# Batch 0's FFN evictions and the maxima of the second mixing get positions of their own, and twelve differences of u move from GpSimd to VectorE

## The chip, the cores and the metric

The kernel runs on one core of a Trainium2 chip. The core has five engines, each with an in-order queue of its own: TensorE (PE) for matrix products, VectorE (DVE), ScalarE (ACT) and GpSimd (POOL) for everything on rows, and SyncE (SP), which here issues the DMAs. Engines wait for each other through semaphores. The metric is the device time of one execution in microseconds (us), the median of several runs.

## The reference

```
scores = scale * q @ k^T - log(S)            # 8 batches, 12 heads, S = 448, head dim 64
x      = sigmoid(scores) @ v                 # back in the shape batch, S, 768
h      = x^T @ U @ V                         # U: 448 x 32, V: 32 x 448, mixes along S
u      = x + h^T
out    = u + relu(u @ w_ch1) @ w_ch2         # 768 -> 3072 -> 768
```

All inputs and the output are float32. The sigmoid attention is followed by a low-rank mixing along the sequence and by an FFN, each with its residual.

## The kernel before

A batch goes through three stages. The attention makes x, kept transposed as six tiles of 128 channels x 448 positions (`ua` for batch 0, `ub` for batch 1 and others). The mixing (`mix`) transposes x (L736), multiplies it by U (L758) and by V (L777) and adds the result to the same tiles, which then hold u. After each addition `largest` (L457) takes the maximum of a tile into `mx`; when all six are there, `mm_u` (L848) reduces them and PE spreads the result over the partitions (L409), from which comes a power-of-two scale. The FFN works in float16 pairs: each operand is split into a high and a low part, and a product is done as three matmuls, hi x hi, hi x lo, lo x hi.

Batches 0 to 3 run the FFN as it stands, in six groups of four hidden slices. `ffn_in` is a chain of 18 matmuls (L914) into a PSUM bank; ACT evicts it twice with a relu (`r`, L921, and the high part `h`, L922), and DVE makes the low part (L923). `ffn_out` is a chain of 12 matmuls (L933) into a bank, which one DVE instruction (a SCALAR_TENSOR_TENSOR of the helper in L393) adds, scaled, to the tile `ua__75` to `ua__80` of u. The two kinds of chain share three banks, 109, 110 and 111, with each other and with the spreading of maxima (L409). So a chain begins when the evictions of the bank's last chain are done.

While batch 0 is in its FFN, much else runs: `decode` brings the weights in, from DMA tiles `w` through ACT (L442), DVE (L393, on 128x768 int32, into `us__88`, `stg` or `at`), a sum on ACT (L453), and high and low parts (L886 on ACT, L393 on DVE) into `w__89` to `w__92`; and batch 1 goes through attention and mixing (`mix(1)`).

Batches 4 to 7 do the FFN in the pairs (4,5) and (6,7) by a scheme of seven products in place of eight on 2x2 blocks. `u_forms` makes the seven left operands from the u of the two batches, for each of three channel thirds c: it loads four blocks and scales them on ACT (L1070), makes the differences t1 to t4 (L1074), casts each operand to its high part on ACT (L1077) and subtracts this for the low part (L1079). `in_quad` multiplies them (L1117), evicts the sums on ACT (L1140) and DVE (L393), and makes the seven operands of the second product by differences (L1146), casts (L1154) and low parts (L1155); `out_quad` multiplies those (L1117 again). For the pair (6,7) the four differences and the low parts of two operands (n = 4 and 6) for each c are on POOL, 18 instructions.

The order of each engine's queue is not written by hand. Every piece of work is given to a `Plan` with an engine, an estimated cost and a position `pos`. `Plan.order` simulates the engines with those costs: an engine that is free takes, among the operations that are ready and have their buffers, the one with the lowest position. `plan.emit()` then writes the instructions in that order, once and for all. A position decides only between operations that are ready at the same simulated time. Evictions of `ffn_in` have the chain's position less `EV_IN` = 29.859, those of `ffn_out` less `EV_OUT` = 5.77.

Of the kernel before, what the change touches and what calls it, by code (L numbers as in the profile page):

```python
# [32 lines left out]
AF = mybir.ActivationFunctionType  # L33
# [35 lines left out]
W_AT, W_STEP, PAIR0, MIX0A, MIX0B, W2_LAG, G0_LEAD = -159.513, 4.417, 4.011, -137.936, -80.644, 0.347, 0.582  # L69
LOW_G = 1  # L70
ORDER = "iiiioiooiioiooiioiooiooo"

# [159 lines left out]
def fused_kernel(ctx: ExitStack, tc: tile.TileContext, q, k, v, wu, wv, w1, w2, out):  # L232
# [474 lines left out]
    def mix(b, pos0, pos1):  # L707
# [61 lines left out]
        for c in range(NP):  # L769
# [6 lines left out]
            else:  # L776
# [3 lines left out]
                    [lp, ku[c], kap], [ku[c]], at)  # L780
            largest(lambda c=c: u32[c].x, lambda c=c: mx.x[:, c : c + 1], [ku[c]], kmx[c], at)
        at += 0.5
# [121 lines left out]
    def ffn_in(b, g, f, pos):  # L904
# [6 lines left out]
        def chain():  # L911
            for c in range(NP):
# [7 lines left out]
        r = plan.tile("r", R)  # L920
        act(0.54, lambda: nc.scalar.activation(r.x, ph.x[:, :S], AF.Relu, scale=DOWN_H), [ph], [r], pos - EV_IN)  # L921
        act(0.54, lambda: nc.scalar.activation(h.x[:, f, 0, :], ph.x[:, :S], AF.Relu, scale=DOWN_H), [ph], [(h, f, 0)], pos - EV_IN)  # L922
        dve2(0.62, lambda: nc.vector.tensor_tensor(out=h.x[:, f, 1, :], in0=r.x, in1=h.x[:, f, 0, :], op=ALU.subtract),  # L923
             [r, (h, f, 0)], [(h, f, 1)], pos - EV_IN)

    def ffn_out(b, g, e, pos):
# [3 lines left out]
        def chain():  # L930
# [9 lines left out]
        dve(0.68, lambda: stt(ku.x, po.x[:, :S], kg.x[:, g : g + 1], ku.x, ALU.mult, ALU.add),  # L940
            [po, (kg, g), ku], [ku], pos - EV_OUT)
        if g == NG - 1:
# [119 lines left out]
    def u_forms(b0, b1, su, pos, after):  # L1062
        fs = {}
        for c in range(3):
# [8 lines left out]
            for o, p_, q_ in ((t1, x[0, 1], x[0, 0]), (t3, x[1, 1], x[0, 1]), (t2, x[1, 1], t1), (t4, x[1, 0], t2)):  # L1073
                pool(1.0, lambda o=o, p_=p_, q_=q_: nc.gpsimd.tensor_tensor(out=o.x, in0=p_.x, in1=q_.x, op=ALU.subtract), [p_, q_], [o], at)  # L1074
            for n, src in ((1, x[0, 0]), (2, x[1, 0]), (3, x[1, 1]), (5, t1), (7, t3), (6, t2), (4, t4)):
                f = fs[n, c] = spot("uf")
                act(0.57, lambda f=f, src=src: nc.scalar.copy(both(f)[:, 0], src.x), [src], [(f, 0)], at)  # L1077
                on_pool = n == 4 or n == 6
                (pool if on_pool else dve2)(1.2 if on_pool else 0.63, lambda f=f, src=src, e=nc.gpsimd if on_pool else nc.vector: e.tensor_tensor(  # L1079
                    out=both(f)[:, 1], in0=src.x, in1=both(f)[:, 0], op=ALU.subtract), [src, (f, 0)], [(f, 1)], at)  # L1080
# [297 lines left out]
```

## Time and profile before

| what | us |
|---|---|
| median of 3 runs | 1559.37 |
| the runs | 1556.81, 1559.37, 1562.81 |
| the profiled execution | 1556.6 |
| its span on the core | 1554.8 |
| PE busy, 0 to 100 us of the span | 91.52 |
| PE busy, 100 to 200 us | 98.51 |
| PE busy, 1300 to 1500 us | 200.00 |
| PE busy, 1500 us to the end | 51.11 of 54.80 |

In this kernel PE is nearly always busy, so time is read from where it is not. In a timeline row the columns are the start and the length in us, the engine, the line, the operation, out<-in with the names of tiles, the sizes, the number of instructions put together (x), and in brackets the idle time just before, with what ended it. Tiles are named by their buffer, which different data use in turn: `stg`, `a`, `w`, `at`, `us__87`, `us__88`, `qk`, `v`, `h` and `r` hold operands of the pair (6,7) late in the program and weights or activations before. A row by stretch gives the window, its length, the busy time and number of instructions of PE, weight loads, DVE, ACT and POOL, then the granted TensorE clock, the DMA share and GB/s.

### The profile page before, as it was taken

To read this page: it belongs to the slowest core of one execution; us is meant where nothing else is said; L and a number is where in the kernel's file an instruction comes from. 1 tells how busy PE (TensorE), PEld (TensorE's weight loads), DVE (VectorE), ACT (ScalarE), POOL (GpSimd) and SP (SyncE) were. 2 spreads that over 40 slices of the span, in tenths; PEclk is the share of its full clock that TensorE was granted. 3 is DMA by queue.
4 is the path that set the end of the run, shared out by engine and by line. 5 is a ranking of instruction groups with operands and counts; after the bars stand their busy time and mean duration, and the time that the engine had idled before them with its cause. 6 is when DMAs were issued, how large, how long until landed. Compare 5 with 4: busy or idle time off the path is not lost.

```text
span 1554.8 us, 24080 instructions
## 1 busy us (share of the span) xinstructions
PE 1524.8 (98%) x8843; PEld 749.9 (48%) x8843; DVE 1118.2 (72%) x1864; ACT 846.9 (54%) x1495; POOL 388.7 (25%) x538
## 2 busy tenths in 40 slices
PE   8999979999999999999999999999999899999999
PEld 3344534544444444444444454555555455555554
DVE  4787898666877768867686856787777667565656
ACT  6788766468867668687686627333332514131310
POOL 1100010642223563312235420055544500000000
PEclk9999999999999999999999999999999999999999
DMA  8877868674665766746766465966566483343331
GB/s 240 270 265 258 265 226 331 233 253 150 154 193 140 236 202 188 186 148 175 239 201 205 161 208 176 308 211 236 201 237 212 145 272 107 117 127 113 107 107 71
DMA packets 184726, 306.02 MB, mean 197 GB/s; under 512 B 54560, under 2 KB 146080, under 8 KB 178464
## 3 DMA queue, kind: packets, MB, share of 16 engines
q1 hardware_dynamic: 184608, 304.49, 61.8%
q8 instruction: 69, 1.13, 0.3%
q14 instruction: 49, 0.40, 0.1%
HBM read 232.88 MB, written 63.26 MB: 190 GB/s over the span
## 4 chain that ended last, share of the span: by engine, by line
PE 86%; DVE 5%; DMA 3%; ACT 3%; issue 1%; POOL 1%; SPq 0%; ACTq 0%; DVEq 0%; POOLq 0%
PE bank L1117 36%; PE bank L933 18%; PE bank L914 18%; PE bank L533 5%; PE bank L552 5%; DMA w<-w_in 3%; DVE stg L393 1%; PE bank L562 1%; PE bank L829 1%; PE bank L537 1%; ACT w L453 1%; DVE us__88 L393 1%; PE bank L838 0%; DVE at L393 0%; DVE w__90 L393 0%
## 5 line engine op out<-in xcount | busy, mean ns | idle before, releaser
L933 PE MATMUL bank<-h__94,w__92 128*128 128x448 f16 x864 | 175.1, 355 | 6.8 <-DVE ua__78 L393 6.8
L933 PE MATMUL bank<-h__93,w__91 128*128 128x448 f16 x864 | 173.5, 353 | 1.9 <-DVE ua__76 L393 1.1
L393 DVE SCALAR_TENSOR_TENSOR a<-at,a 128x896 f16<-128x896 f32 x126 | 137.5, 1112 | 27.5 <-ACT a L679 27.2
L933 PEld LDWEIGHTS <-w__92 128*128 128x128 f16 x864 | 83.0, 98 | 91.0 <-issue 18.6
L914 PEld LDWEIGHTS <-w__89 128*128 128x128 f16 x864 | 83.3, 98 | 84.7 <-issue 8.2
L933 PEld LDWEIGHTS <-w__91 128*128 128x128 f16 x864 | 82.3, 98 | 86.6 <-issue 13.9
L914 PEld LDWEIGHTS <-w__90 128*128 128x128 f16 x864 | 83.8, 98 | 82.0 <-issue 4.8
L679 ACT ACTIVATE a<-at 128x896 f16<-128x896 f32 x126 | 115.5, 960 | 0.6
L1117 PEld LDWEIGHTS <-w__90 128*128 128x128 f16 x756 | 74.4, 98 | 74.7 <-issue 6.7
L976 POOL TENSOR_TENSOR w<-w 128x384 f32<-128x384 f32 x96 | 107.4, 1118 | 5.1
L1117 PEld LDWEIGHTS <-w__92 128*128 128x128 f16 x756 | 74.0, 98 | 69.0
L1117 PEld LDWEIGHTS <-w__89 128*128 128x128 f16 x756 | 74.0, 98 | 69.0
L1117 PEld LDWEIGHTS <-w__91 128*128 128x128 f16 x756 | 74.0, 98 | 68.8
L914 PE MATMUL bank<-us__87,w__89 128*128 128x448 f16 x432 | 84.9, 353 | 2.2 <-DVE ua__78 L393 2.2
L914 PE MATMUL bank<-us__87,w__90 128*128 128x448 f16 x432 | 85.5, 353 | 1.3 <-ACT h__94 L922 1.3
L914 PE MATMUL bank<-us__88,w__89 128*128 128x448 f16 x432 | 85.6, 353 | 0.0
L914 PE MATMUL bank<-us__88,w__90 128*128 128x448 f16 x432 | 85.5, 353 | 0.0
L533 PE MATMUL bank<-stg 64*128 64x448 f16 x648 | 73.8, 351 | 0.0
L972 POOL TENSOR_TENSOR w<-w 128x384 f32<-128x384 f16 x48 | 45.1, 969 | 107.5 <-DVE xnt L984 74.8
L552 PE MATMUL bank<-a,stg 128*64 128x448 f16 x648 | 68.2, 355 | 0.0
L921 ACT ACTIVATE r__95<-bank 128x448 f32<-128x448 f32 x48 | 26.1, 544 | 69.4 <-PE bank L914 69.3
L649 ACT ACTIVATE at<-bank,bias_s,c__216 128x448 f32<-128x448 f32 x72 | 47.2, 726 | 22.8 <-PE bank L533 14.1
(1143 smaller groups left out, 3078.7 us busy)
## 6 DMA issues: line engine op xcount, KB each, us to landing
w<-w_in SPq DMA_DIRECT2D x48, 768.0 KB, 6.3
forms<-xnt SPq DMA_DIRECT2D x24, 768.0 KB, 4.1
w__89<-kept SPq DMA_DIRECT2D x9, 1536.0 KB, 6.5
w__91<-kept SPq DMA_DIRECT2D x9, 1536.0 KB, 9.4
w__90<-kept SPq DMA_DIRECT2D x9, 1536.0 KB, 6.9
w__92<-kept SPq DMA_DIRECT2D x9, 1536.0 KB, 8.3
w__89<-forms SPq DMA_DIRECT2D x12, 768.0 KB, 4.7
w__90<-forms SPq DMA_DIRECT2D x12, 768.0 KB, 5.5
```

Source lines behind the costliest of these rows:

```text
L393: nc.vector.scalar_tensor_tensor(out=out, in0=in0, scalar=s, in1=in1, op0=op0, op1=op1)
L453: act(cost, lambda: nc.scalar.activation((to.x.bitcast(BF16) if to else junk)[:, :n], x(), AF.Abs, accum_out=o()), kx, [ko] + ([to] if to ...
L533: nc.tensor.matmul(sc[j, h].x[:, :S], x[rows_of(h), j * P : j * P + P], y[rows_of(h)], start=i == 0, stop=i == n - 1)
L552: nc.tensor.matmul(av.x[rows_of(h), :S], x[:, j, rows_of(h)], y(tiles[j], h), start=j == 0 and i == 0, stop=not quad and j == 2 and i == n ...
L649: act(cost, lambda: nc.scalar.activation(out_(), in_(), AF.Sigmoid, bias=bias_s, scale=c if whole else by.x), kin + ["bias"] + ([] if whol ...
L679: act(0.95, lambda a=a, to=to: nc.scalar.activation(half(a, 0), to.x, AF.Copy, scale=A_UP), kto, [(a, 0)], here + A_OFF)
L914: nc.tensor.matmul(ph.x[:, :S], w.x[:, f, c, x], us.x[:, c, y, :], start=c == 0 and i == 0, stop=c == NP - 1 and i == 2,)
L921: act(0.54, lambda: nc.scalar.activation(r.x, ph.x[:, :S], AF.Relu, scale=DOWN_H), [ph], [r], pos - EV_IN)
L933: nc.tensor.matmul(po.x[:, :S], w.x[:, f, e, x], h.x[:, f, y, :], start=f == 0 and i == 0, stop=f == FC - 1 and i == 2,)
L972: pool(0.93, lambda j=j: nc.gpsimd.tensor_tensor(out=t.x[:, j], in0=quarter(j, 0), in1=quarter(j, 1), op=ALU.add), [w] if b is None else k ...
L976: pool(1.0, lambda o_=o_, x=x, y=y, sub=sub: nc.gpsimd.tensor_tensor(out=t.x[:, o_], in0=t.x[:, x], in1=t.x[:, y], op=ALU.subtract if sub ...
L1117: nc.tensor.matmul(bank.x[:, :S], wt[1](k, n, x), both(f)[:, y], start=start and k == i == 0, stop=k == 2 and i == 2, skip_group_check=True)
```

## The change

Three constants are added. `EV_IN0` is for batch 0's evictions of `ffn_in` and has the value that `EV_IN` has. `EV_OUT0` puts batch 0's evictions of `ffn_out` at the chain's position less 12.0 instead of less 5.77. `LARGE` puts the six maxima of `mix(1)` 6.0 later than the additions that they follow. In `u_forms`, t1, t2 and t4 and the low part of operand n = 4 go to DVE for each c, 12 instructions in all; t3 and the low part of n = 6 stay on POOL.

```diff
--- before.py
+++ after.py
@@ -68,6 +68,7 @@
 LEAD, SUMS, STEP_K, STEP_I, FFN_LEAD = 13.467, 8.336, 51.271, 26.851, 5.468
 W_AT, W_STEP, PAIR0, MIX0A, MIX0B, W2_LAG, G0_LEAD = -159.513, 4.417, 4.011, -137.936, -80.644, 0.347, 0.582
 LOW_G = 1
+EV_IN0, EV_OUT0, LARGE = 29.859, 12.0, 6.0
 ORDER = "iiiioiooiioiooiioiooiooo"
 
 
@@ -778,7 +779,7 @@
                    [(tt, c // 3), "vst"], [lp], at)
                 dve(0.68, lambda lp=lp, c=c: stt(u32[c].x, lp.x[:, :S], kap.x, u32[c].x, ALU.mult, ALU.add),
                     [lp, ku[c], kap], [ku[c]], at)
-            largest(lambda c=c: u32[c].x, lambda c=c: mx.x[:, c : c + 1], [ku[c]], kmx[c], at)
+            largest(lambda c=c: u32[c].x, lambda c=c: mx.x[:, c : c + 1], [ku[c]], kmx[c], at + (0.0 if whole else LARGE))
         at += 0.5
         if b > 0:
             for c in range(NP):
@@ -918,10 +919,10 @@
 
         entered.append(pe(18 * MM, chain, [(w, 0, f), (w, 1, f)] + [(us, c, x) for c in range(NP) for x in range(2)], [ph], pos, 0.3))
         r = plan.tile("r", R)
-        act(0.54, lambda: nc.scalar.activation(r.x, ph.x[:, :S], AF.Relu, scale=DOWN_H), [ph], [r], pos - EV_IN)
-        act(0.54, lambda: nc.scalar.activation(h.x[:, f, 0, :], ph.x[:, :S], AF.Relu, scale=DOWN_H), [ph], [(h, f, 0)], pos - EV_IN)
+        act(0.54, lambda: nc.scalar.activation(r.x, ph.x[:, :S], AF.Relu, scale=DOWN_H), [ph], [r], pos - (EV_IN if b else EV_IN0))
+        act(0.54, lambda: nc.scalar.activation(h.x[:, f, 0, :], ph.x[:, :S], AF.Relu, scale=DOWN_H), [ph], [(h, f, 0)], pos - (EV_IN if b else EV_IN0))
         dve2(0.62, lambda: nc.vector.tensor_tensor(out=h.x[:, f, 1, :], in0=r.x, in1=h.x[:, f, 0, :], op=ALU.subtract),
-             [r, (h, f, 0)], [(h, f, 1)], pos - EV_IN)
+             [r, (h, f, 0)], [(h, f, 1)], pos - (EV_IN if b else EV_IN0))
 
     def ffn_out(b, g, e, pos):
         u32, w, h, kg = u32s[b], ws[1, b, g], hs[b, g], kgs[b]
@@ -938,7 +939,7 @@
         pe(12 * MM, chain, kw_of(w) + [(h, f, x) for f in range(FC) for x in range(2)], [po], pos, 0.3)
         ku = u32[e]
         dve(0.68, lambda: stt(ku.x, po.x[:, :S], kg.x[:, g : g + 1], ku.x, ALU.mult, ALU.add),
-            [po, (kg, g), ku], [ku], pos - EV_OUT)
+            [po, (kg, g), ku], [ku], pos - (EV_OUT if b else EV_OUT0))
         if g == NG - 1:
             load(lambda: out[b, e], lambda: ku.x, P * S * 4, [ku], [], pos)
 
@@ -1071,11 +1072,13 @@
                 x[r, n] = t
             t1, t2, t3, t4 = (spot("ut") for _ in range(4))
             for o, p_, q_ in ((t1, x[0, 1], x[0, 0]), (t3, x[1, 1], x[0, 1]), (t2, x[1, 1], t1), (t4, x[1, 0], t2)):
-                pool(1.0, lambda o=o, p_=p_, q_=q_: nc.gpsimd.tensor_tensor(out=o.x, in0=p_.x, in1=q_.x, op=ALU.subtract), [p_, q_], [o], at)
+                on_pool = o is t3
+                (pool if on_pool else dve2)(1.0 if on_pool else 0.63, lambda o=o, p_=p_, q_=q_, e=nc.gpsimd if on_pool else nc.vector: e.tensor_tensor(
+                    out=o.x, in0=p_.x, in1=q_.x, op=ALU.subtract), [p_, q_], [o], at)
             for n, src in ((1, x[0, 0]), (2, x[1, 0]), (3, x[1, 1]), (5, t1), (7, t3), (6, t2), (4, t4)):
                 f = fs[n, c] = spot("uf")
                 act(0.57, lambda f=f, src=src: nc.scalar.copy(both(f)[:, 0], src.x), [src], [(f, 0)], at)
-                on_pool = n == 4 or n == 6
+                on_pool = n == 6
                 (pool if on_pool else dve2)(1.2 if on_pool else 0.63, lambda f=f, src=src, e=nc.gpsimd if on_pool else nc.vector: e.tensor_tensor(
                     out=both(f)[:, 1], in0=src.x, in1=both(f)[:, 0], op=ALU.subtract), [src, (f, 0)], [(f, 1)], at)
         return fs
```

In the changed program all lines behind the constants are one higher, those of `u_forms` behind its differences two or three.

On DVE, where batch 1's second half of the mixing is done. Names are as above: `ub` is u of batch 1, `mx` its maxima, `us__88` and `stg` of 128x768 weights being decoded. Before:

```order
L393 SCALAR_TENSOR_TENSOR us__88<-w_107,us__88 128x768 x2
L393 SCALAR_TENSOR_TENSOR ub__84<-bank_113,kap__198,ub__84 128x448
L393 SCALAR_TENSOR_TENSOR ub__85<-bank_112,kap__198,ub__85 128x448
L457 TENSOR_REDUCE mx__154<-ub__84 128x1
L457 TENSOR_REDUCE mx__154<-ub__85 128x1
L393 SCALAR_TENSOR_TENSOR ub__86<-bank_115,kap__198,ub__86 128x448
L393 SCALAR_TENSOR_TENSOR us__88<-w_107,us__88 128x768
L457 TENSOR_REDUCE mx__154<-ub__86 128x1
L393 SCALAR_TENSOR_TENSOR us__88<-w_107,us__88 128x768
L848 TENSOR_REDUCE mm_u__157<-mx__154 128x1
L393 SCALAR_TENSOR_TENSOR ua__78<-bank_110,kg__168,ua__78 128x448
L393 SCALAR_TENSOR_TENSOR stg<-w_107,stg 128x768
```

Now:

```order
L458 TENSOR_REDUCE mx__154<-ub__84 128x1
L458 TENSOR_REDUCE mx__154<-ub__85 128x1
L458 TENSOR_REDUCE mx__154<-ub__86 128x1
L924 TENSOR_TENSOR h__94<-r__96,h__94 128x448
L849 TENSOR_REDUCE mm_u__157<-mx__154 128x1
L394 SCALAR_TENSOR_TENSOR us__88<-w_107,us__88 128x768
L394 SCALAR_TENSOR_TENSOR ua__77<-bank_110,kg__168,ua__77 128x448
L394 SCALAR_TENSOR_TENSOR us__88<-w_107,us__88 128x768 x2
L394 SCALAR_TENSOR_TENSOR ua__78<-bank_111,kg__168,ua__78 128x448
L394 SCALAR_TENSOR_TENSOR us__88<-w_107,us__88 128x768
L394 SCALAR_TENSOR_TENSOR stg<-w_107,stg 128x768
L394 SCALAR_TENSOR_TENSOR ua__79<-bank_109,kg__168,ua__79 128x448
```

The last maxima now stand together ahead of `mm_u`. The four `us__88` decodes of the first piece stood ahead of it and now follow it, with the evictions of `ua__77` and `ua__78` between them; the two earlier `us__88` decodes of this weight, further up, keep their side. The eviction of `ua__77` stood 39 rows further up and now is the first behind `mm_u`.

On PE, in the FFN of batch 0 while batch 1's attention is multiplied (L552 and L562 before, L553 and L563 now). Before, around the second of two chains of `ffn_in`:

```order
L914 MATMUL bank_109<-us__87,w__89 128x448
L933 LDWEIGHTS w__92
L933 MATMUL bank_110<-h__94,w__92 128x448
...
L914 MATMUL bank_111<-us__87,w__89 128x448
...
L552 MATMUL bank_116<-a,v__105 64x448 x6
L562 MATMUL bank_115<-a,v__104 64x448 x2
L562 MATMUL bank_116<-a,v__105 64x448 x2
L933 LDWEIGHTS w__92
L933 MATMUL bank_109<-h__94,w__92 128x448
```

Now:

```order
L915 MATMUL bank_109<-us__87,w__89 128x448
L934 LDWEIGHTS w__92
L934 MATMUL bank_110<-h__94,w__92 128x448
...
L915 MATMUL bank_109<-us__87,w__89 128x448
...
L553 MATMUL bank_116<-a,v__105 64x448 x6
L563 MATMUL bank_115<-a,v__104 64x448 x2
L563 MATMUL bank_116<-a,v__105 64x448 x2
L410 MATMUL bank_111<-ident,mm_w__174 128x128
L934 LDWEIGHTS w__92
L934 MATMUL bank_110<-h__94,w__92 128x448
```

The second chain of `ffn_in` has changed from bank 111 to bank 109, that of the chain of `ffn_in` before it; the spreading of `mm_w__174` now comes ahead of the next chain and has bank 111.

On DVE, where the operands of the pair (6,7) are made. Before:

```order
L1079 TENSOR_TENSOR h__94<-w_107,h__94 128x448
L393 SCALAR_TENSOR_TENSOR stg<-bank_112,fg,us__87 128x448
L1079 TENSOR_TENSOR a<-r__96,a 128x448
L393 SCALAR_TENSOR_TENSOR qk__100<-bank_114,fg,stg 128x448
L393 SCALAR_TENSOR_TENSOR qk__101<-bank_109,fg,qk__100 128x448
L393 SCALAR_TENSOR_TENSOR stg<-bank_114,fg,stg 128x448
L393 SCALAR_TENSOR_TENSOR us__87<-qk__101,us__87 128x448
L393 SCALAR_TENSOR_TENSOR a<-bank_109,fg,stg 128x448
L1170 TENSOR_TENSOR v__104<-v__102,v__104 128x448
L393 SCALAR_TENSOR_TENSOR stg<-bank_110,kg__241,stg 128x448
L393 SCALAR_TENSOR_TENSOR us__87<-stg,us__87 128x448
L1146 TENSOR_TENSOR a<-a,v__102 128x448
```

Now:

```order
L1076 TENSOR_TENSOR a<-at,us__87 128x448
L1076 TENSOR_TENSOR us__87<-w_107,a 128x448
L1082 TENSOR_TENSOR a<-r__96,a 128x448
L394 SCALAR_TENSOR_TENSOR qk__99<-bank_116,fg,us__87 128x448
L394 SCALAR_TENSOR_TENSOR qk__100<-bank_113,fg,qk__99 128x448
L1076 TENSOR_TENSOR qk__99<-r__96,us__87 128x448
L394 SCALAR_TENSOR_TENSOR w_107<-bank_109,fg,qk__100 128x448
L1082 TENSOR_TENSOR a<-a 128x448
L1082 TENSOR_TENSOR h__93<-stg,h__93 128x448
L394 SCALAR_TENSOR_TENSOR v__102<-w_107,v__102 128x448
L1082 TENSOR_TENSOR us__87<-qk__99,us__87 128x448
L1076 TENSOR_TENSOR v__105<-h__93,us__88 128x448
```

L1074 becomes L1076 and L1079 becomes L1082. Four differences of u and one low part of n = 4 (into `us__87`) now stand in this piece between the evictions of the quad, and L1146's counterpart follows six rows further on; POOL's piece of 18 instructions has six.

## The prediction

> **What bounds the kernel now.** I read the totals by engine first, then the busy time of each engine by stretch, then TensorE's waits, then the timelines of the engines around the long ones.
>
> ```profile
> span 1554.8 us, 24080 instructions
> PE 1524.8 (98%) x8843; PEld 749.9 (48%) x8843; DVE 1118.2 (72%) x1864; ACT 846.9 (54%) x1495; POOL 388.7 (25%) x538
> 200.00:300.00 100.00, 87.62 (x451) 44.32 (x450) 81.80 (x146) 57.36 (x94) 26.61 (x33) 0.97 0.71 260
> 300.00:1200.00 900.00, 900.00 (x5615) 442.70 (x5614) 669.22 (x1095) 542.91 (x952) 327.93 (x461) 1.00 0.65 201
> 1200.00:1300.00 100.00, 96.04 (x498) 49.05 (x497) 69.64 (x115) 37.39 (x71) 20.82 (x18) 0.98 0.59 195
> ```
>
> TensorE (PE) is busy for 1524.8 of 1554.8 us, so 30.0 us of idle time is what reordering can win, and little beside it. In a row by stretch, the columns behind the length are PE, weight loads, VectorE (DVE), ScalarE (ACT), GpSimd (POOL) and the granted clock. From 300 to 1200 PE never idles. It idles 12.4 us in 200–300 and 4.0 us in 1200–1300, the two places that the change touches; the rest lies ahead of them and at the end.
>
> ```profile
> PE bank L933 <- DVE ua__78 L393: 6.8, 1, 6.8
> PE bank L1117 <- ACT a L1154: 3.3, 1, 3.3
> PE bank L914 <- DVE ua__78 L393: 2.2, 1, 2.2
> ```
>
> These are PE's longest waits at these places (total, times, longest). Those for `ua__78` lie in batch 0's FFN and make 9.0 of the 12.4: a bank is held until DVE evicts it into `ua` (L393). L1117 is the first quad of the pair (6,7).
>
> **The second place: differences of u on DVE.** I take it first, since its chain of releases can be followed row by row.
>
> ```profile
> 1230.02 0.73 PE L1117 MATMUL bank<-h__93,w__90 128*128 128x448 f16 x3
> 1230.59 0.73 PE L1117 MATMUL bank<-us__88,w__90 128*128 128x448 f16 x3
> 1234.62 0.35 PE L1117 MATMUL bank<-a,w__90 128*128 128x448 f16 x1 [3.30 <-ACT a L1154]
> 1235.63 0.54 PE L1117 MATMUL bank<-a,w__90 128*128 128x448 f16 x2 [0.66 <-DVE a L1155]
> ...
> 1239.28 0.84 PE L1117 MATMUL bank<-h__94,w__90 128*128 128x448 f16 x3
> 1239.95 0.73 PE L1117 MATMUL bank<-a,w__90 128*128 128x448 f16 x3
> ```
>
> ```profile
> 1224.59 0.57 ACT L1140 ACTIVATE a<-a 128x448 f32<-128x448 f32 x1
> 1228.97 1.54 DVE L1146 TENSOR_TENSOR a<-a,v__102 128x448 f32<-128x448 f32 x1 [2.02 <-POOL stg L1074]
> 1233.52 0.57 ACT L1154 CAST v__105<-a 128x448 f16<-128x448 f32 x1 [1.42 <-POOL qk__100 L1079]
> 1234.43 0.61 DVE L1155 TENSOR_TENSOR v__105<-a,v__105 128x448 f16<-128x448 f32 x1
> 1234.96 0.61 DVE L1155 TENSOR_TENSOR a<-stg,a 128x448 f16<-128x448 f32 x1
> 1232.46 1.02 POOL L1079 TENSOR_TENSOR qk__100<-v__105,qk__100 128x448 f16<-128x448 f32 x1
> ```
>
> POOL's 18 u instructions end at 1233.48. DVE and ACT wait for its results, and the casts and differences that PE needs next (L1146, L1154, L1155) are queued behind those waits. At full pace a group of three matmuls starts 0.57 after the last, or 0.189 for each matmul. PE's unblocked work ends with the group at 1230.59, at 1231.16. From there to 1239.95 it does the 15 matmuls of the rows from 1234.62 to 1239.28: 15 × 0.189 = 2.83, and 8.79 were taken. So **5.96 us** are lost: 3.96 in the two waits, 2.0 in a seam and in slow matmuls behind them.
>
> The change takes 12 of the 18 off POOL. One lasts 1.02 (1232.46) or more there; on DVE this shape lasts 0.61 with the next start 0.53 later (1234.43, 1234.96), so DVE gets 12 × 0.53 = 6.4 us. What hides them is time in which DVE waits for PE:
>
> ```profile
> 1205.00:1231.00 26.00, 26.00 (x139) 13.33 (x137) 14.70 (x22) 19.52 (x38) 18.33 (x16) 1.00 0.61 198
> 1236.00:1256.00 20.00, 20.00 (x98) 9.97 (x97) 19.19 (x35) 0.56 (x1) 0.00 (x0) 0.91 0.62 198
> 1256.00:1266.00 10.00, 10.00 (x55) 5.18 (x53) 5.79 (x9) 0.00 (x0) 0.00 (x0) 1.00 0.93 322
> ```
>
> POOL's other 16 fill 18.3 of the 26 us to 1231, while DVE is free for 11.3. In the changed order six of the twelve stand ahead of the quad's first difference (L1146): 3.2 us, which fit. That difference no longer stands behind a POOL result; its other operand was started on ACT at 1224.59, so it can run near 1226, and the blocked operands (two casts, about six DVE steps of 0.6) are there by 1229 to 1230, before PE asks at 1231.16. What is late next is then nothing of POOL's: the six it keeps take some 7 of the 26 us.
>
> The other six fall into 1236–1256, where DVE had 0.8 us free. If that fullness were all real, 6 × 0.53 = 3.2 us would come back as waits for banks before the 4.2 free in 1256–1266 take them up. But part of it is backlog of the stall, and PE did not wait there though DVE was behind. The gain lies between 5.96 − 3.2 = 2.8 and 5.96; I take **5.7**, near the upper end, since the row nearest to the case is that PE's time in 1236–1256 is 20.0 of 20.
>
> A rule speaks against this move. The Trainium skill, "SBUF — State Buffer", section "Who interferes with whom", says that a DVE instruction with two SBUF inputs and a GpSimd instruction that reads SBUF exclude each other for a whole instruction. The row at 1228.97 agrees: 1.54 on DVE instead of 0.61, with POOL at work. By the rule a moved instruction beside one of POOL's six could be 0.93 longer, at most 5.6 in all, inside the free 11.3; the sum would stay.
>
> **The first place: evictions and maxima in batch 0's FFN.** `EV_IN0` equals `EV_IN`, so the evictions of `ffn_in` keep their positions, at no cost. `EV_OUT0` puts batch 0's `ffn_out` evictions 6.23 earlier by position, `LARGE` six maxima 6.0 later. Nothing is added; only the order changes.
>
> ```profile
> 207.77 1.82 DVE L393 SCALAR_TENSOR_TENSOR us__88<-w,us__88 128x768 int32<-128x768 int32 x2
> 214.59 0.15 DVE L848 TENSOR_REDUCE mm_u__157<-mx__154 128x1 f32<-128x6 f32 x1
> 214.66 0.67 DVE L393 SCALAR_TENSOR_TENSOR ua__78<-bank,kg__168,ua__78 128x448 f32<-128x448 f32 x1
> 215.39 4.15 PE L933 MATMUL bank<-h__94,w__92 128*128 128x448 f16 x12 [6.78 <-DVE ua__78 L393]
> 219.37 0.27 PE L409 MATMUL bank<-ident,mm_u__157 128*128 128x128 f32 x1
> ```
>
> The 6.78 wait ends with the eviction behind `mm_u__157`, and the 12 matmuls after it take 3.98 instead of 2.27: together 8.5 us. In the changed order the eviction still stands behind the maxima and `mm_u`. But of the six `us__88` decodes ahead of `mm_u` four now follow it, one of them ahead of the eviction, which is now that of `ua__77`, and an earlier `ua` eviction is gone from in front. At about 0.9 a decode and 0.6 an eviction, it comes 3 × 0.87 + 0.6 = 3.2 earlier.
>
> That would be 3.2 to 4.9 us (4.9 if the slow matmuls go too). But the decodes put off must be done before `w__91` can be:
>
> ```profile
> 160.00:248.00 88.00, 76.98 (x406) 39.06 (x405) 80.90 (x153) 63.14 (x115) 7.71 (x15) 0.96 0.78 253
> 220.00:248.00 28.00, 25.80 (x139) 13.39 (x137) 27.12 (x54) 19.86 (x33) 5.08 (x7) 1.00 0.65 226
> DVE us__88 L393 <- ACT us__88 L442: 2.2, 1, 2.2
> DVE ua__75 L393 <- PE bank L933: 1.3, 1, 1.3
> 244.27 3.81 DVE L393 SCALAR_TENSOR_TENSOR w__91<-stg,s_w__183,w__91 128x768 f16<-128x768 f32 x4 [0.38 <-ACT w__91 L886]
> 247.04 7.28 PE L933 MATMUL bank<-h__93,w__91 128*128 128x448 f16 x36
> ```
>
> Up to `w__91` DVE does the same instructions before and after, but for one that moves ahead of it. It ends that tile at 248.08, and PE begins to use it at 247.04: at this mark PE is as late as DVE lets it be. From 160 to 248 DVE has 7.1 us free, and by DVE's own waits the longest piece of it is one for a decode on ACT (2.2), which the change doesn't hasten. Only the 1.3 for `ua__75` belongs to the stretch that gets better. So the net gain is 0 to 1.3, with 7.1 as the far end; behind `w__91` both orders run nearly alike, and what PE waits there stays. Against it stands a new wait:
>
> ```profile
> 159.45 3.57 PE L914 MATMUL bank<-us__87,w__89 128*128 128x448 f16 x18
> 161.22 1.00 ACT L442 ACTIVATE stg<-w,minus 128x768 f32<-128x768 uint16 x1 [0.79 <-DMA w<-w_in]
> 162.12 0.52 ACT L921 ACTIVATE r__95<-bank 128x448 f32<-128x448 f32 x1
> 162.55 0.53 ACT L922 ACTIVATE h__93<-bank 128x448 f16<-128x448 f32 x1
> ```
>
> The chain at 159.45 had bank 111; it now gets bank 109, which ACT frees with the two evictions ending at 163.08, behind a decode that waits for a load. That is a stall of 2.0 (if ACT comes sooner) to 4.2 us (one attention activation is now ahead too), with 0 to 1.7 of slow matmuls by the 215.39 row. It costs nothing as long as PE would have waited later anyway, and 9.0 us of waits follow. I take **0.8** as the gain of this place, from +7.1 down to −5.9.
>
> The 1.7 has a rule beside it. The Trainium skill, "TensorE: Matmul & The Clock Gate", section "Part 1: The HAM clock gate", has the clock halved after an idle window of about 3.4 us. The 6.78 wait agrees; by it a stall of 4.2 would have slow matmuls behind it, one of 2.0 none.
>
> **Sum.** The profiled execution took 1556.6, 1.8 more than its span. 1556.6 − 5.7 − 0.8 = 1550.1. The median of the runs is 1559.37, 2.8 above it, and I keep that distance: **1552.9**.
>
> **Rivals.** *Both places win in full.* If the order in batch 0 also frees DVE, by its 7.1, the time is 1559.4 − 5.96 − 7.1 = 1546.3. PE's 12.4 us of idle time speak for it, the full DVE in 220–248 against.
>
> *The new wait isn't absorbed: slower.* PE stands at 159.45 for 4.2, runs slow for 1.7, and the attention behind it (L552) and so DVE's first steps of the mixing come 5.9 later. If DVE runs dry for it, which it does once its decodes on hand are fewer than 5.9 us of work, `w__91` comes 5.9 later and the second place pays only 2.8: 1559.4 + 5.9 − 2.8 = 1562.5. The waits for ACT and for a load show that such gaps occur; against it, DVE is free for only 0.9 us in 220–248, so its decodes on hand are many.
>
> *The second place gives only 2.8*, the six later instructions holding up the quad's evictions: 1559.4 − 2.8 − 0.8 = 1555.8.
>
> **Chances.** The forecast 0.47, both in full 0.29, only 2.8 at the second place 0.12, the new wait 0.12. The range leaves out half of the second and half of the last: 1546.5 to 1562.0. A measurement can tell about 0.5%, 7.8 us, from no change: faster means under 1551.6. That takes in the case of full gains and a fifth of the forecast's own spread: 0.38. Slower, over 1567.2, needs the new wait and more: 0.06. The rest is 0.56.
>
> **What would show it.** Right: no PE wait at L1117 in 1200–1300, L1146's counterpart near 1220 to 1226 with no wait for POOL, and PE idle under 0.5 us there; in 200–300 still 10 us or more of PE idle, in more and smaller waits; a new wait for ACT's `h__93` near 160. Wrong: PE idle of 200–300 under 6 us (then DVE was not the bound there), or DVE waits of 3 us and more for PE in 160–205.

## The result

The changed kernel took 1549.38 us as the median of five runs (1547.32 to 1552.89), the kernel before 1556.81 in the same comparison (1556.34 to 1562.81). The ratio is 0.9944 with a 95% interval of 0.9924 to 0.9963: faster by 0.56%, or 8.7 us by the ratio (5.8 to 11.8). The prediction said 1552.9 within 1546.5 to 1562.0, a gain of 6.5.

The profiled execution of the changed kernel is the longest of its five, 1552.89 with a span of 1551.1, so its span is only 3.7 under that of before. The stretches show why. Rows by stretch of the changed kernel, columns as above:

```profile
0.00:100.00 100.00, 90.30 (x414) 34.79 (x416) 61.98 (x117) 69.77 (x129) 10.34 (x19) 0.98 0.81 248
100.00:200.00 100.00, 95.68 (x512) 45.86 (x509) 80.29 (x138) 82.70 (x152) 2.42 (x8) 0.98 0.79 262
200.00:300.00 100.00, 92.41 (x474) 46.03 (x473) 82.90 (x153) 59.12 (x98) 25.92 (x32) 0.98 0.74 267
1200.00:1300.00 100.00, 100.00 (x531) 51.69 (x530) 77.78 (x133) 39.63 (x75) 6.59 (x6) 1.00 0.64 206
```

TensorE has no idle time left in 1200–1300. It gained 4.8 us of busy time in 200–300 but lost 2.8 in 100–200 and 1.2 in the first hundred. Up to 113 us the change touches nothing: every engine has the same order there in both kernels. To take the start out I use two marks that stand in both PE timelines, the 24 matmuls into `ffn_out` after 100 us and the first chain of batch 1. Of before, then of the changed kernel (what counts is where the rows start; the window of the view cuts the second ones off):

```profile
109.28 4.71 PE L933 MATMUL bank<-h__93,w__91 128*128 128x448 f16 x24
278.03 5.27 PE L914 MATMUL bank<-us__88,w__89 128*128 128x448 f16 x27
```

```profile
112.25 4.71 PE L934 MATMUL bank<-h__93,w__91 128*128 128x448 f16 x24
280.42 2.81 PE L915 MATMUL bank<-us__88,w__89 128*128 128x448 f16 x14
```

The profiled execution of the changed kernel was 2.97 us late at the first mark already. **Stretch A**, between the marks, holds all of batch 0's change: 168.75 before, 168.17 now. **Stretch B**, from the second mark to the end of the span, holds the differences of u: 1554.8 − 278.03 = 1276.77 before, 1551.1 − 280.42 = 1270.68 now, 6.09 less.

PE's waits in the changed kernel (total, times, longest), the longest of batch 0's FFN; L915 and L934 are the chains of `ffn_in` and `ffn_out`:

```profile
PE bank L915 <- ACT h__93 L923: 2.5, 1, 2.5
PE bank L915 <- ACT h__94 L923: 1.5, 2, 1.1
PE bank L915 <- ACT stg L443: 1.5, 1, 1.5
PE bank L934 <- DVE ua__77 L394: 1.4, 1, 1.4
PE bank L934 <- ACT w__91 L887: 1.3, 1, 1.3
PE bank L934 <- ACT h__94 L923: 1.1, 1, 1.1
```

The waits of 6.8 and 2.2 for `ua__78` are gone, and no row at L1120, the quads, is left. In their place stand smaller waits, and the largest is the one that the prediction named, for ACT's `h__93`. On PE's timeline:

```profile
160.15 2.43 PE L934 MATMUL bank<-h__94,w__92 128*128 128x448 f16 x12
165.12 5.04 PE L915 MATMUL bank<-us__87,w__89 128*128 128x448 f16 x18 [2.54 <-ACT h__93 L923]
215.97 2.43 PE L934 MATMUL bank<-h__93,w__91 128*128 128x448 f16 x12 [1.35 <-DVE ua__77 L394]
247.82 0.55 PE L934 MATMUL bank<-h__93,w__91 128*128 128x448 f16 x2 [1.30 <-ACT w__91 L887]
```

The 18 matmuls behind the 2.54 wait took 5.04 instead of 3.57. And what ACT did, whose decode waited 3.1 us for its load:

```profile
162.69 0.98 ACT L443 ACTIVATE stg<-w,minus 128x768 f32<-128x768 uint16 x1 [3.14 <-DMA w<-w_in]
```

At the second place, DVE's timeline with the quad's first difference (L1149 now) and two of the moved instructions (L1076), and then POOL's:

```profile
1219.43 1.31 DVE L1076 TENSOR_TENSOR qk__99<-r__96,us__87 128x448 f32<-128x448 f32 x1
1226.25 0.61 DVE L1076 TENSOR_TENSOR a<-a,v__105 128x448 f32<-128x448 f32 x1
1227.58 0.63 DVE L1149 TENSOR_TENSOR stg<-a,v__103 128x448 f32<-128x448 f32 x1 [0.18 <-ACT a L1143]
```

```profile
1219.12 1.14 POOL L1076 TENSOR_TENSOR qk__100<-a,h__93 128x448 f32<-128x448 f32 x1
1228.55 1.09 POOL L1082 TENSOR_TENSOR qk__99<-a,qk__99 128x448 f16<-128x448 f32 x1 [2.21 <-ACT qk__99 L1080]
```

PE stands 2.39 us later here than before (280.42 against 278.03). L1149 at 1227.58 is therefore 1225.2 on the clock of before, where it ran at 1228.97 after a wait for POOL. It now waits for ACT alone.

### The profile page after: what moved, and what is told of

Same layout as the page of the kernel before. It is cut to its first block, busy times and chain, and to the rows that moved or that the text cites. A ratio compares the mean times of both kernels' runs of the same rounds, so it can differ in the third digit from the quotient of the medians.

```text
span 1551.1 us, 24076 instructions
## 1 busy us (share of the span) xinstructions
PE 1525.8 (98%) x8843; PEld 748.8 (48%) x8843; DVE 1121.5 (72%) x1876; ACT 848.0 (55%) x1495; POOL 372.8 (24%) x526
## 4 chain that ended last, share of the span: by engine, by line
PE 89%; DVE 6%; DMA 2%; issue 1%; ACT 1%; SPq 0%; ACTq 0%; DVEq 0%
PE bank L1120 37%; PE bank L915 19%; PE bank L934 19%; PE bank L534 5%; PE bank L553 5%; DMA w<-w_in 2%; DVE stg L394 1%; PE bank L563 1%; PE bank L830 1%; PE bank L538 1%; DVE us__88 L394 1%; DVE at L394 1%; PE bank L839 0%; DVE w__89 L394 0%; DVE w__90 L394 0%
## 5 line engine op out<-in xcount | busy, mean ns | idle before, releaser
L934 PE MATMUL bank<-h__93,w__91 128*128 128x448 f16 x864 | 175.0, 355 | 5.9 <-DVE ua__77 L394 1.4
L934 PE MATMUL bank<-h__94,w__92 128*128 128x448 f16 x864 | 173.1, 353 | 0.0
L934 PEld LDWEIGHTS <-w__91 128*128 128x128 f16 x864 | 82.2, 98 | 91.9 <-issue 15.5
L915 PEld LDWEIGHTS <-w__89 128*128 128x128 f16 x864 | 83.7, 98 | 86.5 <-issue 11.6
L915 PEld LDWEIGHTS <-w__90 128*128 128x128 f16 x864 | 83.8, 98 | 84.1 <-issue 7.6
L934 PEld LDWEIGHTS <-w__92 128*128 128x128 f16 x864 | 82.5, 98 | 82.9 <-issue 9.6
L1120 PEld LDWEIGHTS <-w__90 128*128 128x128 f16 x756 | 74.0, 98 | 69.0
L1120 PEld LDWEIGHTS <-w__92 128*128 128x128 f16 x756 | 74.0, 98 | 69.0
L1120 PEld LDWEIGHTS <-w__89 128*128 128x128 f16 x756 | 74.0, 98 | 69.0
L1120 PEld LDWEIGHTS <-w__91 128*128 128x128 f16 x756 | 74.0, 98 | 68.8
L915 PE MATMUL bank<-us__87,w__89 128*128 128x448 f16 x432 | 86.6, 357 | 2.8 <-ACT h__93 L923 2.5
L915 PE MATMUL bank<-us__87,w__90 128*128 128x448 f16 x432 | 85.5, 352 | 3.0 <-ACT h__94 L923 1.5
L915 PE MATMUL bank<-us__88,w__89 128*128 128x448 f16 x432 | 85.6, 353 | 0.0
L915 PE MATMUL bank<-us__88,w__90 128*128 128x448 f16 x432 | 85.5, 353 | 0.0
L553 PE MATMUL bank<-a,stg 128*64 128x448 f16 x648 | 68.2, 355 | 0.0
```

What stands on the lines that cost most here:

```text
L553: nc.tensor.matmul(av.x[rows_of(h), :S], x[:, j, rows_of(h)], y(tiles[j], h), start=j == 0 and i == 0, stop=not quad and j == 2 and i == n ...
L915: nc.tensor.matmul(ph.x[:, :S], w.x[:, f, c, x], us.x[:, c, y, :], start=c == 0 and i == 0, stop=c == NP - 1 and i == 2,)
L934: nc.tensor.matmul(po.x[:, :S], w.x[:, f, e, x], h.x[:, f, y, :], start=f == 0 and i == 0, stop=f == FC - 1 and i == 2,)
L1120: nc.tensor.matmul(bank.x[:, :S], wt[1](k, n, x), both(f)[:, y], start=start and k == i == 0, stop=k == 2 and i == 2, skip_group_check=True)
```

## The experiments

Each is compared with the kernel before on the same chip. "Ratio" is of the runs to those of before, with its 95% interval; A and B are the stretches of the profiled execution, and "h__93" is PE's wait in A for those two evictions.

| kernel | median us | before us | ratio | A | h__93 | B |
|---|---|---|---|---|---|---|
| before | | | | 168.75 | none | 1276.77 |
| changed | 1549.38 | 1556.81 | 0.9944 [0.9924, 0.9963] | 168.17 | 2.54 | 1270.68 |
| after_again | 1549.92 | 1559.81 | 0.9939 [0.9919, 0.9960] | 167.95 | 2.11 | 1270.65 |
| u_only | 1552.91 | 1558.93 | 0.9962 [0.9949, 0.9976] | 170.29 | none | 1270.65 |
| order_only | 1555.58 | 1558.93 | 0.9985 [0.9973, 0.9997] | 164.33 | none | 1277.46 |
| evict_only | 1556.95 | 1558.93 | 0.9989 [0.9980, 0.9999] | 165.78 | none | 1277.31 |
| maxima_only | 1562.21 | 1558.93 | 1.0023 [1.0009, 1.0037] | 172.29 | none | 1277.30 |
| free_first | 1549.51 | 1559.81 | 0.9930 [0.9910, 0.9950] | 163.98 | none | 1270.71 |
| twice_max | 1555.23 | 1559.81 | 0.9972 [0.9957, 0.9987] | 170.50 | none | 1270.70 |
| all_dve | 1550.83 | 1559.81 | 0.9933 [0.9912, 0.9953] | 170.83 | 3.86 | 1270.64 |
| subs_only | 1548.20 | 1558.57 | 0.9943 [0.9921, 0.9964] | 166.29 | 1.80 | 1270.63 |
| lo_only | 1548.74 | 1558.57 | 0.9940 [0.9918, 0.9962] | 164.99 | 0.57 | 1270.75 |
| h_pool | 1549.11 | 1558.57 | 0.9944 [0.9927, 0.9961] | 167.80 | none | 1270.69 |
| half_loads | 1549.85 | 1559.06 | 0.9949 [0.9932, 0.9965] | 163.98 | none | 1270.71 |

B is the same to 0.12 us wherever the u part is in. A is that of one execution and differs between executions of one order (168.75 and 170.29 for the order of before); why is the subject of half of the runs. The first mark itself lies between 108.58 (`subs_only`) and 116.21 us (`free_first`), so the start, which the change doesn't touch, spreads the times as much as A does.

### The two parts alone

The second part alone, `u_only`:

```diff
-EV_IN0, EV_OUT0, LARGE = 29.859, 12.0, 6.0
+EV_IN0, EV_OUT0, LARGE = 29.859, 5.77, 0.0
```

> Only the twelve instructions of u_forms move; batch 0's positions are those of before. Two stretches are read in the trace, apart from the first 110 us, where the start differs from run to run: A, from the 24 matmuls into the first ffn_out after 100 us (109.28 before, 112.25 in the changed kernel) to the first ffn_in of batch 1 (278.03 and 280.42): 168.75 before, 168.17 in the changed kernel; B, from there to the end of the span: 1276.77 and 1270.68. My theory: A as before, 168.75 within 0.3; B 1270.7; no PE wait at the quads of the pair (6,7); the median 6 us under before. Rival, that the gain of the two parts is not a sum because the queues of both parts hang together: B between 1271.5 and 1276.

B came out at 1270.65, as in the changed kernel, with no wait at the quads. The ratio is worth 5.9 us (3.7 to 8.0). A, 170.29, was 1.5 longer than the 168.75 of the same order before, outside the 0.3 expected. The wait of 2.21 at L914 is in both, but the 36 matmuls behind it took 8.49 us here and 6.81 before, 1.7 more (rows in the last section).

The first part alone, `order_only`, with `u_forms` as before:

```diff
-                on_pool = o is t3
+                on_pool = True
...
-                on_pool = n == 6
+                on_pool = n == 4 or n == 6
```

> Only EV_OUT0 and LARGE; u_forms as before. My theory (DVE sets the end of stretch A): A 168.2 within 0.5, B as before, 1276.8, with the waits of 3.3 and 0.7 at the quad; the median 0 to 2 us under before. Rival (the evictions placed apart win the stretch): A under 165 and the median 4 us or more under before, the u part then being worth less than 4.

The ratio is worth 2.3 us (0.5 to 4.2); the medians are 3.35 apart. Both points lie between the theory's 0 to 2 and the rival's 4 or more, and the interval takes in parts of each. A, 164.33, is 4.4 under before, outside the theory's 168.2 ± 0.5 and inside the rival's "under 165". The waits at the quads stay, 3.3 and 0.5. PE's order around the second `ffn_in` chain is that of the changed kernel, but here ACT's load came in time, and there was no wait for `h__93`. PE's timeline, then ACT's:

```profile
159.90 2.43 PE L934 MATMUL bank<-h__94,w__92 128*128 128x448 f16 x12
162.48 3.57 PE L915 MATMUL bank<-us__87,w__89 128*128 128x448 f16 x18
```

```profile
160.04 1.01 ACT L443 ACTIVATE stg<-w,minus 128x768 f32<-128x768 uint16 x1 [0.95 <-DMA w<-w_in]
```

So the two parts multiply to 0.9962 × 0.9985 = 0.9947, and the changed kernel has 0.9944 and 0.9939: within the intervals the gain is the sum of two. The first part's 2.3 is more than the 0.8 forecast, but its interval reaches down to 0.5.

### Evictions and maxima apart

Both start from `order_only`. `evict_only`:

```diff
-EV_IN0, EV_OUT0, LARGE = 29.859, 12.0, 6.0
+EV_IN0, EV_OUT0, LARGE = 29.859, 12.0, 0.0
```

> Only EV_OUT0 = 12, maxima and u_forms as before. My theory: the evictions make the new order (second ffn_in chain on bank 109, ua__77 right behind mm_u), so A is that of both, 168.2 within 1.0, with the new wait of about 2.5 for ACT's h__93; the maxima are worth under 1 us. Rival (the maxima carry it): A 170 or more, later than before, since the eviction then stands behind decodes as well.

A 165.78 and a ratio worth 1.7 us (0.2 to 3.1): the evictions make the new order, and against the 2.3 of `order_only` the maxima add nothing that the intervals can tell. The wait expected for `h__93` did not come, since the loads were in time.

`maxima_only`:

```diff
-EV_IN0, EV_OUT0, LARGE = 29.859, 12.0, 6.0
+EV_IN0, EV_OUT0, LARGE = 29.859, 5.77, 6.0
```

> Only LARGE = 6, evictions and u_forms as before. My theory: PE's chains keep the banks of before (second ffn_in chain on bank 111), so there is no wait for ACT's h__93 near 160, and the long wait for ua__78 stays: A 168 to 170. Rival (the maxima ahead of mm_u set the long wait): that wait falls from 6.8 to under 3.5 and A to under 167.

The banks stay and the wait for `ua__78` stays, as the theory said, but the kernel is slower than before, by 3.6 us (1.4 to 5.8), and A is 172.29, above either expectation. PE's waits show what it costs:

```profile
PE bank L934 <- DVE ua__78 L394: 7.8, 1, 7.8
PE bank L934 <- ACT w__91 L887: 4.6, 1, 4.6
```

Later maxima by themselves don't put off `mm_u` (102.8 us after the first mark, 105.3 before), but two decodes now stand between it and the eviction of `ua__78`, and that wait is 1.0 longer. PE then reaches `w__91` 140.2 after the mark instead of 137.8; why that tile is late was not followed up. Together with the earlier evictions they did not lose: 0.9985 against 0.9989, the same within the intervals.

### The wait for h__93

`after_again` is the changed kernel once more.

> The changed kernel once more, beside the three below. Sum of the two parts measured alone, 0.9962 x 0.9985 = 0.9947, so the median 8 us under before (6 to 10). In the trace stretch A is between 164 and 168.5, by whether PE stands for ACT's h__93 near 160 or not, and B 1270.7.

It came in as expected. `free_first` moves one instruction of its ACT queue, with no other row of any queue changed. `behind` holds the decode of group 3's last piece of `w_ch1`, `last` the second eviction of group 2's third chain; the decode is moved in the finished list:

```diff
-        for i in self.order():
+        done = self.order()
+        for i in self.behind:
+            a, b = done.index(i), done.index(self.last)
...
+            done.insert(b, done.pop(a))
+        for i in done:
```

> The changed kernel with one ACT instruction put three places later: the weight decode L443 into stg, which waits for a load, now comes behind the two evictions of the bank that the second ffn_in chain needs (and behind one attention activation). Everything else has its place. My theory as predicted (the wait is absorbed, since DVE sets the end of the stretch): no wait for h__93 near 160, yet A and the median as in the changed kernel within 1 us. Rival (the wait is not absorbed, as two traces now say, with A 168.17 with it and 164.33 without): A 164 to 165.5 in the trace, the median 1 to 3 us under the changed kernel's.

The wait is gone and A is 163.98, 4 us less than in the two executions with the wait: the rival's value. Its 1 to 3 us in the median did not come: 1549.51 against 1549.92 is less than the runs can tell, so most runs probably have a shorter wait than those two profiles. The executions of this order line up by the wait: 163.98 without, 164.99 with 0.57, 166.29 with 1.80, 167.95 with 2.11, 168.17 with 2.54, 170.83 with 3.86. Nothing of it is absorbed.

The wait follows the load. ACT's decode into `stg` started 48.45 us after the first mark in `lo_only`, 49.70 in `subs_only`, 50.02 in `after_again`, 50.44 in the changed kernel and 51.76 in `all_dve`, and each time PE's wait is that less 47.9, within 0.02. ACT's timeline in `all_dve`:

```profile
163.59 1.00 ACT L443 ACTIVATE stg<-w,minus 128x768 f32<-128x768 uint16 x1 [1.00 <-DMA w<-w_in]
```

Where it started at 48.03 or before (`order_only`, `evict_only`, `twice_max`, `half_loads`), no wait is shown. In `free_first` the load, issued at 154.98, landed 9.4 us later, 48.2 after the mark, so at its old place too the decode would have cost PE only some 0.3. That execution shows A without the wait, not that the move is worth 4 us, and the equal medians fit that.

### What bounds stretch A

`twice_max` gives DVE 3.2 us more, in an unchanged order:

```diff
-        dve(0.61, lambda: nc.vector.tensor_reduce(...),
+        dve(0.61, lambda: [nc.vector.tensor_reduce(...) for _ in range(times)],
```

> The changed kernel, but each of the six maxima of the second mixing is taken twice on DVE, in place: 6 x 0.53 = 3.2 us more work for DVE ahead of mm_u and of w__91, in an unchanged order. My theory (DVE is the bound of stretch A): A and the median 2.5 to 3.5 us longer than in the changed kernel. Rival (PE, ACT and the loads bound it, DVE has idle time that takes the work up): 0 to 1.2 us longer.

A is 170.50, 6.5 over the 163.98 of the same order without the wait for `h__93`, and the median 5.3 over that of `after_again`. That is more than DVE was given, and more than the 2.5 to 3.5 expected. PE's timeline has the rest:

```profile
215.45 4.64 PE L934 MATMUL bank<-h__93,w__91 128*128 128x448 f16 x12 [4.03 <-DVE ua__77 L394]
219.89 5.06 PE L934 MATMUL bank<-h__94,w__92 128*128 128x448 f16 x24
```

The wait for `ua__77` grew from 1.35 to 4.03, and the matmuls behind it ran slow: the first twelve took 4.44 to the next start instead of 2.27. The wait for `xnt` at L778 grew from 0.19 to 1.49. Together these are some 6.2 of the 6.5. So DVE's queue ahead of `ua__77` has no slack. That less work there would help doesn't follow. `h_pool` takes 24 instructions off DVE, at their old places in the order:

```diff
-        dve2(0.62, lambda: nc.vector.tensor_tensor(out=h.x[:, f, 1, :], ...
+        dve2(0.62, lambda: (nc.vector if b else nc.gpsimd).tensor_tensor(out=h.x[:, f, 1, :], ...
```

> The kernel of free_first with the 24 low parts of batch 0's hidden values (L924) issued on POOL in place of DVE, at the same places of the order: 24 x 0.53 = 12.7 us less for DVE over batch 0's FFN, some ten of them in stretch A, at 1.1 us each on POOL, which is nearly idle there. My theory (DVE is the bound of stretch A: 3.2 us more cost 5 to 6): A falls from 164.0 to 158 to 161.5 and the median to 3 to 6 us under that of free_first, 1549.5. Rival (ACT and the loads are as near a bound): A 162.5 to 164.5. Second rival (the slower low parts hold up ffn_out): A over 165.

A is 167.80, where the second rival had it, but the median is 1549.11 and the ratio 0.9944, no gain over `free_first` and no loss that the intervals can tell. In this execution DVE's idle time in A grew to 26.3 us, against 20.6 in `free_first`, with waits such as these:

```profile
DVE stg L400 <- ACT stg L449: 3.6, 5, 2.3
DVE mx__154 L464 <- ACT ub__83 L696: 2.9, 1, 2.9
DVE xnt L400 <- ACT xnt L758: 2.4, 2, 1.6
DVE w__91 L400 <- ACT w__91 L895: 2.4, 2, 1.2
```

DVE freed of work waited for ACT. But ACT waited for loads too, 11.7 us between 110 and 245 against 7.6 in `free_first`, so this A doesn't tell a bound by ACT from late loads. Last, `half_loads` halves the weight loads from the third group on, in an unchanged order:

```diff
-                    return src[g, :, n * PIECE : (n + 1) * PIECE]
+                    return src[g, :, n * PIECE : (n + 1) * PIECE - (PIECE // 2 if g >= 2 else 0)]
```

> The changed kernel in an unchanged order, but from the third of the six weight groups on each load of weights into w brings half of its columns, and the other half is decoded from what lies there (part of the weights is left out, so the output is not the reference's). My theory: the loads set how early ACT's decodes (L443) run, and these how early DVE's; with half the bytes ACT waits for loads under 1 us in all between 110 and 245, no wait for h__93 near 160, and A falls from 164.0 (168 with that wait) to 158 to 162; the median 2 to 5 us under the changed kernel's. Rival (once the loads are on time, the chain of decodes, evictions and maxima on DVE and ACT sets the stretch): A 163 to 164.5, that is, only the wait for h__93 goes, the median 0 to 1.5 us under.

Between 110 and 245 ACT waits for no load any more, and A is 163.98, to a hundredth that of `free_first`, where ACT still waited 7.6 us for loads. So loads cost the new order's stretch A only through `h__93`; without that wait it is 164.0, the rival's value. That the chain of decodes, evictions and maxima on ACT and DVE sets the 164.0 is argued: it is what is left. The ratio, 0.9949, shows no gain over the changed kernel's 0.9944 and 0.9939.

### How much had to leave POOL

`all_dve` moves the other six too:

```diff
-                on_pool = o is t3
+                on_pool = False
...
-                on_pool = n == 6
+                on_pool = False
```

> The changed kernel with t3 and the low part of n = 6 on DVE as well, so that POOL has none of u_forms' instructions: 6 x 0.53 = 3.2 us more for DVE around the quad. My theory: DVE's free time takes it up, PE waits at no quad, B 1270.7 within 0.5 and the median that of the changed kernel. Rival (the six left on POOL are what keeps DVE's queue short enough): PE waits for banks at the quads of (6,7), B 1272 to 1274.

B 1270.64, no wait at a quad: DVE takes all 18. `subs_only` leaves the low parts of n = 4 on POOL:

```diff
-                on_pool = n == 6
+                on_pool = n == 4 or n == 6
```

> The changed kernel, but the low parts of n = 4 stay on POOL; only nine differences (t1, t2, t4) go to DVE, and POOL has nine instructions. My theory (POOL's length was the bound; nine instructions are some 10 us, well inside the quad's 26): no PE wait at the quad, B 1270.7 within 0.4. Rival (every instruction on POOL that stands ahead of the quad's casts on ACT delays them): B 1271.5 to 1273.

B 1270.63, as the theory said. `lo_only` leaves all differences there:

```diff
-                on_pool = o is t3
+                on_pool = True
```

> The changed kernel, but all differences stay on POOL; only the three low parts of n = 4 go to DVE, and POOL has 15 instructions. My theory: POOL ends some 3 x 1.1 = 3.3 us earlier than before's 18, so most of the wait at the quad is left or gone by 3.3: B between 1272.5 and 1274.5. Rival (only the low parts count, since their results stood last): B 1270.7.

B is 1270.75: three instructions moved win as much as twelve or eighteen. That is the rival's value, which the theory had excluded. The timelines of POOL, DVE and PE there:

```profile
1225.45 1.42 POOL L1082 TENSOR_TENSOR a<-stg,a 128x448 f16<-128x448 f32 x1
```

```profile
1227.81 0.61 DVE L1158 TENSOR_TENSOR stg<-h__93,stg 128x448 f16<-128x448 f32 x1
1228.34 0.61 DVE L1158 TENSOR_TENSOR r__96<-us__88,r__96 128x448 f16<-128x448 f32 x1
```

```profile
1226.19 0.73 PE L1120 MATMUL bank<-h__94,w__91 128*128 128x448 f16 x3
1231.87 0.73 PE L1120 MATMUL bank<-r__96,w__90 128*128 128x448 f16 x3
```

The second mark is at 273.65 in this execution, 4.38 earlier than before. POOL ends at 1226.87, which is 1231.25 on the clock of before, 2.2 earlier than 1233.48; the first operand (`stg`, L1158) is done at 1228.42, and PE would have asked for it at 1231.16 − 4.38 = 1226.78. That would still be a wait of 1.6. But the planner has also put other groups at this point of PE's queue, among them `w__91` at 1226.19, and PE comes to `r__96` only at 1231.87, 2.9 us after it is done. So the instructions moved and PE's new order did it together; they were not tried apart.

## Why the prediction was right

**The sum.** Predicted was a gain of 6.5, measured 7.4 by the medians and 8.7 by the ratio. Of the 3.5 us between 1552.9 and 1549.38, 2.6 lie in the kernel before, which had 1559.37 as the median of three runs and 1556.81 of five. The time, 1549.38, lies almost as near the rival "both places in full" (1546.3) as the forecast; by the gain, 8.7 within 5.8 to 11.8, the forecast's 6.5 is inside and the rival's 13.1 is not.

**The second place: right, in mechanism and size.** 5.7 was taken of 5.96; B fell by 6.09, and `u_only` gained 5.9 (3.7 to 8.0). DVE's free time hid what was added, as L1149's place shows. The lower end, 2.8, by a DVE that holds up the evictions in what was 1236–1256, is excluded by B, and by `all_dve`, which loads DVE more and loses nothing. The rule of the Trainium skill, "SBUF — State Buffer", section "Who interferes with whom", agrees with the trace: the moved instruction at 1219.43 lasted 1.31 beside POOL's at 1219.12, the one at 1226.25, as POOL fell idle, lasted 0.61, and PE waited for neither. What the prediction had not seen is that far fewer instructions would do.

**The first place: right that little would change in the profile, wrong in two steps.** The first is that the new wait for `h__93` "costs nothing as long as PE would have waited later anyway". It came, with 2.54 inside the forecast 2.0 to 4.2 and slow matmuls behind it, and the executions above show that all of it passes to the end of the stretch: A is 4.2 longer with it than without.

The second is the reading of `w__91`, "at this mark PE is as late as DVE lets it be". The row at 247.04 has no wait, and DVE had begun the tile at 244.27: PE, after its waits of 6.78 and 2.21, was 2.8 us behind what DVE allowed. In the new order PE does wait for the tile. DVE in the changed kernel (PE's row is the one at 247.82 above), then DVE and PE in `free_first`:

```profile
247.80 3.80 DVE L394 SCALAR_TENSOR_TENSOR w__91<-stg,s_w__183,w__91 128x768 f16<-128x768 f32 x4 [1.19 <-ACT w__91 L887]
```

```profile
247.57 3.81 DVE L400 SCALAR_TENSOR_TENSOR w__91<-stg,s_w__183,w__91 128x768 f16<-128x768 f32 x4 [1.19 <-ACT w__91 L895]
247.60 0.55 PE L944 MATMUL bank<-h__93,w__91 128*128 128x448 f16 x2 [1.30 <-ACT w__91 L895]
```

Counted from the first mark, PE reaches the tile at 137.76 before, 135.57 in the changed kernel and 131.39 in `free_first`; DVE begins it at 134.99, 135.55 and 131.36. So in the changed kernel PE gained 2.2 up to `w__91` although DVE was no sooner, and lost 1.6 of it again behind the tile, where the prediction had both orders "run nearly alike".

In `free_first` DVE itself is 3.6 sooner, although the prediction saw in its idle time only waits "which the change doesn't hasten". DVE's waits for decodes on ACT before `w__91` were 6.3 us in the kernel before, the first rows; then the two longest waits of `free_first` and what is left there of those for decodes:

```profile
DVE stg L393 <- ACT stg L442: 2.3, 2, 1.8
DVE us__88 L393 <- ACT us__88 L442: 2.2, 1, 2.2
DVE at L393 <- ACT at L442: 1.8, 1, 1.8
```

```profile
DVE e_w__177 L419 <- PE bank L416: 2.9, 2, 1.8
DVE e_w__179 L419 <- PE bank L416: 2.7, 1, 2.7
DVE stg L400 <- ACT stg L449: 1.2, 2, 0.9
```

Those waits became 1.2, and DVE's idle time from the first mark to `w__91` went from 18.1 to 14.6. But ACT's decodes came sooner there too. Its second decode into `us__88` ended 50.1 us after the mark before and 46.6 in `free_first`:

```profile
158.39 1.00 ACT L442 ACTIVATE us__88<-w,minus 128x768 f32<-128x768 uint16 x1 [2.95 <-DMA w<-w_in]
```

```profile
160.88 1.88 ACT L449 ACTIVATE us__88<-w,minus 128x768 f32<-128x768 uint16 x2
```

In both executions of the old order the loads were late (the decode into `stg` started 51.9 after the mark). In the new order DVE's waits for decodes are 1.0 to 1.2 in most executions, but 6.0 in `all_dve`, whose load was as late, and DVE's idle time in the changed kernel was 18.7. So it stays open how much comes from evictions that take the places ahead of waiting decodes, and how much from loads in time. What is shown is the size: the term was put at 0.8 and measured 2.3 (0.5 to 4.2) by `order_only`. That A fell by 168.75 − 168.17 = 0.58 in the profiled execution, near the 0.8, is luck: with its load in time the same order has 164.0.

**DVE as the bound** was half right. `twice_max` shows that work added ahead of `ua__77` is paid for more than once; `h_pool` shows by its median that work taken away elsewhere buys nothing; that ACT is next is not shown. "In 200–300 still 10 us or more of PE idle" failed too: it was 7.6.

**The slower rival** priced the wait at 4.2 + 1.7 with no absorption. That nothing is absorbed is right, and the price was low: 6.85 for a wait of 3.86 in `all_dve`, where the slow matmuls took 2.8 more. But it comes only where the load is late, and the medians are faster all the same.

## What to carry to other kernels

Where engines share a few banks, look at what stands at the head of the evicting engine's queue: moving evictions to earlier places and maxima to later ones gained 2.3 us here (0.5 to 4.2), though the engine had the same instructions to do. An operation put behind a transfer in an in-order queue makes everything behind it depend on when the load lands, so put the eviction that a matrix product waits for ahead of it. And before moving a whole set of instructions to another engine, try the few that stand last: three of twelve, with the order that the planner made for them, were enough here.

## What was not expected of the hardware

How long a wait must be for slow matmuls behind it. The same 18 matmuls (L915) ran at full pace after waits of 0.57 and 1.80 and slow after 2.11, 2.54 and 3.86:

```profile
160.70 3.56 PE L915 MATMUL bank<-us__87,w__89 128*128 128x448 f16 x18 [1.80 <-ACT h__93 L923]
```

```profile
167.13 5.25 PE L915 MATMUL bank<-us__87,w__89 128*128 128x448 f16 x18 [2.11 <-ACT h__93 L923]
```

The first is of `subs_only`, the second of `after_again`. In the changed kernel the granted clock was 0.55 in the 3.4 us behind the wait of 2.54. But the length alone doesn't decide. The same wait of 2.21 ahead of the same 36 matmuls cost no pace in the kernel before (233.31 to 240.12, 0.189 each), and 1.7 us in `u_only` (238.33 to 246.82):

```profile
233.31 6.97 PE L914 MATMUL bank<-us__87,w__89 128*128 128x448 f16 x36 [2.21 <-DVE ua__78 L393]
```

```profile
238.33 8.65 PE L915 MATMUL bank<-us__87,w__89 128*128 128x448 f16 x36 [2.21 <-DVE ua__78 L394]
```

What tells the two apart is not shown. The prediction's bounds, no loss at 2.2 and a full one at 6.8, were too far apart, and the lower one held in one execution of two. The Trainium skill, "TensorE: Matmul & The Clock Gate", section "Part 1: The HAM clock gate", has an idle window of about 3.4 us, and the waits of 2.11, 2.21 and 2.54 lie under that; here the measurement decides.

Not settled: whether the order of before would also reach an A of 164 with its loads in time, and why loads come later in some executions; neither was tried.
